# A start in a new order: whole weight rows in one transfer, and landmark sums that begin on GpSimd

## The chip, the cores and the metric

The kernel runs on one core of a Trainium2 chip. The metric is the device time of one execution in microseconds. TensorE (PE), VectorE (DVE), ScalarE (ACT) and GpSimd (POOL) each work through a queue of their own in order; SyncE (SP) issues the transfers.

## The reference

Three stages follow one another: attention with 32 landmarks (Nystrom), then two MLP layers. `w_in` and `w_out` are float64, the rest float32.

```
q, k, v: (4, 8, 576, 64)            # batch, heads, tokens, head width
q_lm, k_lm = means of q, k over 18 neighbouring tokens      # 32 landmarks
A, Bm, C = softmax(q k_lm'), softmax(q_lm k_lm'), softmax(q_lm k')
Z = Bm' / (norm1(Bm) * norminf(Bm) + 1e-6)
6 times: Z = 2 Z - Z Bm Z                                  # Newton
x = (A Z C v) as (2304 tokens, 512)
x = mish(x @ w_in) @ w_out          # 512 -> 2048 -> 512
x = relu(x @ w2_in)**2 @ w2_out     # 512 -> 2048 -> 512
```

## The kernel before

The whole kernel is one list of steps, `PROGRAM`, written out in order. Each step names a thing and a method (`b.sk` is method `sk` of group b); behind @ stands the kind of PSUM tile that the step takes, and `+n` puts n products of the identity with itself on TensorE before it (line 257). Each step issues instructions on one engine, and each engine works through its own in the order of the list; a step waits by semaphore for what it reads and for the buffer that it writes.

*Attention.* a to h are eight groups, each four heads of one of four batches (a, b: batch 0; c, d: batch 1; e to h: batches 2 and 3). `lk`, `lq`, `lv` load k, q and v; every landmark takes 18 tokens, so a partition holds 18 x 64 values. `sk`, `sq` sum the 18 on VectorE (line 471; c to f, whose loads come in two tiles, in two steps, lines 465 and 471), `Sk`, `Sq` copy the sum, `tk`, `tq`, `tl` transpose, `Tk`, `Tq`, `TL` copy that out of PSUM. `pb`, `pc`, `pa` are the score products, `cm ce cr` and `am mi ae su mu` the softmaxes of C and A, `at`, `tb` transposes of A, `ah`, `al` A's high and low part, `pe ET pv cv` the product of C with v.

*Newton.* B0, B1, B2 take a and b, c and d, e to h. `bx be bs nr rs` prepare, `n0` to `n5` are the six rounds on TensorE, each with `r` on ScalarE and `z` on VectorE before the next; `pw`, `wz` multiply the result with `cv`.

*Weights.* U0, U1, ... are units of 128 x 512 float64 values: for each quarter of a layer's 2048 columns four of w_in, then four of w_out (U0 to U3, U4 to U7, and so on). `d` loads a unit, `lo st ab cl ad` build float32 from its two words (ScalarE, VectorE, ScalarE or VectorE, VectorE, GpSimd), `hi`, `lw` split w_out's into a high and a low part. A w_in unit of layer 1 consists of the 64 rows of head c and of head 4 + c, each loaded by a transfer of its own (line 317).

*Layer 1.* Since x = A (Z C v), `w_in` is first multiplied with Z C v: fold `Fbf` (`fo`, line 826; `mh`, `ml`) for batch b and a quarter f of the 2048 columns. A fold is eight products of 64 rows on eight pieces of the array: its two halves of rows (64 each) times its four groups of 32 columns; `g` picks the half of rows and the PSUM bank. Turns t0 to t23 take 384 tokens and a quarter: `f` multiplies A with the fold, `M` is mish, `c`, `g` split, `y` multiplies with w_out, `e` adds up. All such products are made of three, from high and low parts. t0 reads F00 alone, t1 reads F00 and F10.

*Layer 2* (W, K, X, Q, Y, Z steps) follows.

Of the kernel before, what the change touches and what calls it, by code (L numbers as in the profile page):

```python
# [23 lines left out]
LM = 32
SEG = 18
NPB = SEG // 2
# [36 lines left out]
    t0.e0 f.Sk d.su U9.d U11.lo t0.y1 d.mu e.cm f.tl@at t0.e1 f.TL e.ce t0.y2 f.pa@at U11.st c.tb f.at F10.fo@h  # L63
    U11.ab c.ah d.tb f.pc@h e.pa@at t0.e2 f.pb@y f.cm g.lk U11.cl g.lq t0.y3 c.al F10.mh f.ce d.ah d.al F10.ml
    e.pe@h U9.lo e.at U11.ad t0.e3 U9.st U9.ab e.lv U9.cl U9.ad e.ET e.am t1.f0 t1.f1 t1.M0 t1.f2 t1.f3 t1.c0
    g.tk@at g.sk U10.d t1.M1 t2.f0 f.cr g.Tk g.sq t1.g0 t1.c1 g.Sq f.am e.mi f.PB U10.lo t2.f1 U10.st g.tq@at t2.f2
    t1.g1 g.lv t2.M0 g.Sk U10.ab t1.y0 f.pe@h e.ae U13.d U10.cl t1.y1 U10.ad t1.e0 U13.lo e.su U13.st t2.f3 h.lv
# [1321 lines left out]
```

## Time and profile before

| | us |
|---|---|
| time, median of three runs | 791.8 |
| lowest and highest | 791.39, 794.12 |
| span of the profiled execution | 788.7 |
| TensorE busy in it | 764.8 |
| VectorE busy in it | 600.2 |
| GpSimd busy in it | 383.5 |

The profile follows one execution: its span is from its first to its last instruction; a time of its own for that execution, with what lies around the span, is not given, so the median of the runs stands beside it. A busy TensorE is not TensorE at its peak. Idle time of an engine counts only where another waits for that engine.

### The profile page before, as it was taken

The page shows a single profiled execution, that of the slowest core. Times are in us where ns is not written, and L with a number is a line of the kernel's source. Part 1 is how long each engine was busy: PE and PEld are TensorE (multiplying, and loading weights), DVE is VectorE, ACT ScalarE, POOL GpSimd, SP SyncE. Part 2 cuts the span into 40 slices and gives each one's busy share as a digit, 9 for nine tenths or more (in the row PEclk, how much of TensorE's full clock was granted, in tenths as well). Part 3 has the DMA queues.
Part 4 walks back from the last instruction along what each step waited for, and adds up shares of the span by engine and source line. Part 5 has one row for each costly group of instructions (what it writes and reads, how often), then busy time and mean ns, then how long its engine had stood idle before and what let it go on. Part 6 is the DMA issues. An engine that isn't in the chain of part 4 may idle for free.

```text
span 788.7 us, 15310 instructions
## 1 busy us (share of the span) xinstructions
PE 764.8 (97%) x5878; PEld 713.4 (90%) x5878; DVE 600.2 (76%) x937; ACT 369.0 (47%) x582; POOL 383.5 (49%) x273
## 2 busy tenths in 40 slices
...
GB/s 273 299 152 55 205 172 105 58 54 32 103 54 107 121 166 172 190 209 213 205 233 233 248 277 254 259 278 269 265 282 336 351 248 236 218 227 317 329 63 80
DMA packets 87783, 156.71 MB, mean 199 GB/s; under 512 B 9376, under 2 KB 37024, under 8 KB 87712
## 3 DMA queue, kind: packets, MB, share of 16 engines
...
q10 hardware_dynamic: 576, 0.79, 0.4%
...
## 4 chain that ended last, share of the span: by engine, by line
PE 87%; DMA 6%; DVE 4%; ACT 1%; issue 1%; SPq 0%; POOL 0%; DVEq 0%; ACTq 0%; POOLq 0%
PE y L841 8%; PE y L843 8%; PE y L842 8%; PE P L1221 7%; PE P L1222 7%; PE P L1223 7%; DMA rawwi<-in_moe_w_in_dram 4%; PE O L842 4%; PE O L843 4%; PE O L841 4%; PE h L841 4%; PE h L842 4%; PE h L843 4%; PE O L1289 4%; PE O L1290 4%; PE O L1288 3%
## 5 line engine op out<-in xcount | busy, mean ns | idle before, releaser
L1117 POOL TENSOR_TENSOR glr<-A,ghr 128x768 fp32r<-128x768 f32 x49 | 100.3, 2067 | 69.5 <-ACT ghr L1112 69.3
L842 PE MATMUL O<-b,ghr 128*128 128x256 f32 x294 | 83.1, 283 | 0.3 <-DMA b<-sc 0.3
L843 PE MATMUL O<-b,glr 128*128 128x256 f32 x294 | 83.0, 282 | 0.0
L841 PE MATMUL O<-b,ghr 128*128 128x256 f32 x294 | 82.9, 282 | 0.0
L841 PE MATMUL h<-ah,mh 128*128 128x384 f32 (+1 forms) x256 | 78.7, 307 | 0.0
L843 PE MATMUL h<-ah,ml 128*128 128x384 f32 (+1 forms) x256 | 77.9, 304 | 0.0
L842 PE MATMUL h<-al,mh 128*128 128x384 f32 (+1 forms) x256 | 77.9, 304 | 0.0
L1112 ACT CAST ghr<-A 128x768 fp32r<-128x768 f32 x49 | 40.3, 837 | 78.7 <-DVE A L1094 30.2
L955 DVE TENSOR_TENSOR acc<-acc,y 128x384 f32<-128x384 f32 x72 | 39.1, 549 | 42.9 <-PE y L843 42.9
L1251 DVE TENSOR_TENSOR U<-U,P 128x384 f32<-128x384 f32 x72 | 39.7, 552 | 30.7 <-PE P L1223 29.2
L842 PEld LDWEIGHTS O<-b,ghr 128*128 128x128 f32 x294 | 56.0, 191 | 0.6 <-DMA b<-sc 0.6
L843 PEld LDWEIGHTS O<-b,glr 128*128 128x128 f32 x294 | 56.1, 191 | 0.0
L841 PEld LDWEIGHTS O<-b,ghr 128*128 128x128 f32 x294 | 55.9, 190 | 0.0
L914 DVE TENSOR_TENSOR gl<-s,gh 128x768 fp32r<-128x768 f32 x48 | 51.7, 1080 | 3.9 <-ACT gh L904 3.9
L893 ACT ACTIVATE s<-h 128x768 f32<-128x768 f32 x48 | 39.0, 813 | 30.8 <-DVE gl L914 18.1
L841 PEld LDWEIGHTS h<-ah,mh 128*128 128x128 f32 x256 | 48.5, 190 | 3.9 <-issue 1.7
L843 PEld LDWEIGHTS h<-ah,ml 128*128 128x128 f32 x256 | 48.6, 190 | 0.0
L842 PEld LDWEIGHTS h<-al,mh 128*128 128x128 f32 x256 | 48.6, 190 | 0.0
L904 ACT CAST gh<-s 128x768 fp32r<-128x768 f32 x48 | 39.6, 836 | 13.8 <-PE y L843 13.5
L1251 DVE TENSOR_TENSOR A<-U,P 128x384 f32<-128x384 f32 x56 | 30.4, 550 | 20.0 <-PE P L1223 17.6
L348 POOL TENSOR_TENSOR wi<-rawwi 128x512 int32<-128x512 int32 x16 | 18.3, 1148 | 54.6 <-DVE rawwi L342 31.2
L1231 ACT COPY U<-P 128x384 f32<-128x384 f32 x24 | 11.5, 478 | 64.5 <-PE P L1223 50.1
...
## 6 DMA issues: line engine op xcount, KB each, us to landing
b<-sc SPq DMA_DIRECT2D x98, 256.0 KB, 4.5
...
rawwi<-in_moe_w_in_dram SPq DMA_DIRECT2D x48, 256.0 KB, 4.2
...
sc<-sh SPq DMA_DIRECT2D x16, 256.0 KB, 5.0
```

Of the source, the lines that this page charges most:

```text
L841: nc.tensor.matmul(ps, wh, rh, start=start, stop=False)
L842: nc.tensor.matmul(ps, wh, rl, start=False, stop=False)
L843: nc.tensor.matmul(ps, wl, rh, start=False, stop=stop)
L904: nc.scalar.copy(gh, s)
L914: nc.vector.tensor_tensor(self.gl[:, sl, :], self.s[hf], self.gh[:, sl, :].bitcast(F32), ALU.subtract)
L955: nc.vector.tensor_tensor(a, a, ps, ALU.add)
L1112: nc.scalar.copy(self.form(k)[0], self.A[self.src(k)])
L1117: nc.gpsimd.tensor_tensor(lo, self.A[self.src(k)], hi.bitcast(F32), ALU.subtract)
L1221: nc.tensor.matmul(ps[:, :TT], wh[:, c], xh[:, c, :], start=c == 0, stop=False)
L1222: nc.tensor.matmul(ps[:, :TT], wh[:, c], xl[:, c, :], start=False, stop=False)
L1223: nc.tensor.matmul(ps[:, :TT], wl[:, c], xh[:, c, :], start=False, stop=c == 1)
L1251: nc.vector.tensor_tensor(to, x, self.ps[i][:, :TT], ALU.add)
```

## The change

A w_in unit of layer 1 becomes 128 rows in one transfer, so that it holds heads 2c and 2c + 1. `fo` takes its rows accordingly (half of rows `e`, bank `g`), `pw` writes its result in the matching layout with twice as many products of half the width, and `pa` writes group 1's heads in swapped places. New steps `hk`, `hq` add the three thirds of the 18 tokens on GpSimd, and the sum on VectorE then reads 384 values a partition; b to f have both, a, g and h have none. The `+n` come to 23 products where they were 35. The first 1240 steps, now 1250, stand in a new order; the other 1320 are as they were.

The list below is cut after the first product `t0.y0` of either order.

```diff
@@ PROGRAM @@
-    a.lq a.lk b.lk U1.d@m U0.d@m b.lq a.sq a.tq@h d.lq a.Tq a.sk a.tk@h a.Sq a.Sk a.tl@y b.sk U2.d@m a.Tk a.TL
-    a.pa@at U1.lo U4.d U1.st a.pb@y a.pc@h U7.d@gl a.PB b.Sk a.at U0.lo c.lk b.tk@h a.cm a.am a.ce U0.st a.mi b.Tk
-    b.tq@h b.sq U1.ab U0.ab c.lq a.pe@at U1.cl b.Sq b.Tq d.sq b.tl@y U1.ad U3.d@m U2.lo b.TL b.pc@h+4 a.cr a.ET
-    U0.cl U4.lo a.lv U2.st b.pb@at U4.st b.PB b.pa@at B0.bx b.cm B0.be U4.ab c.tk@h+3 a.ae B0.bs U7.lo U6.d@gh U4.cl
-    b.ce d.lk B0.nr@y b.at d.tq@h B0.rs c.tq@at+2 d.Tq b.lv a.su c.Tq b.am U3.lo e.lk B0.n0@at+5 U7.st b.mi c.sq
-    B0.r0 U4.ad c.Tk U2.ab c.Sq B0.z0 c.sk U3.st B0.n1@y B0.r1 B0.z1 b.pe@h a.pv@y B0.n2@at+2 U0.ad U7.ab d.tk@h
-    a.mu c.Sk a.cv b.ET U3.ab B0.r2 U2.cl a.tb c.tl@y b.ae U3.cl B0.z2 d.Sq d.sk c.TL B0.n3@y+2 B0.r3 c.pb@at a.ah
-    U7.cl B0.z3 U3.ad U5.d b.pv@y+1 U6.lo d.Sk c.pc@h b.cr d.Tk c.cm U2.ad B0.n4@y b.cv B0.r4 e.tk@h B0.z4 d.tl@y
-    B0.n5@y c.PB b.su f.lk B0.z5 c.pa@at c.at B0.pw@y+3 U4.hi c.ce c.am B0.wz U7.ad d.TL e.lq a.al U7.hi U7.lw
-    d.pc@at d.lv b.mu d.cm e.Tk b.tb d.ce c.mi d.pb@y e.sq F00.fo@h F00.mh d.pe@at F00.ml f.tk@h+4 U6.st d.PB U4.lw
-    b.ah U5.lo B1.bx d.ET f.lq B1.be f.Tk b.al d.pa@at t0.f0 c.ae t0.f1 d.at B1.bs d.cr B1.nr@y U5.st U6.ab U8.d
-    U5.ab B1.rs t0.M0 c.su t0.f2 U6.cl d.am t0.f3 c.lv B1.n0@y+2 B1.z0 d.pv@y U8.lo U6.ad c.pe@h e.Sq B1.r0 t0.c0
-    e.sk U8.st B1.n1@y B1.z1 f.tq@at t0.M1 e.tq@h d.mi t0.g0 U6.hi B1.r1 B1.n2@y d.cv c.ET B1.z2 U5.cl U5.ad f.Tq
-    B1.r2 e.Tq B1.n3@y+4 B1.r3 c.pv@y c.cr e.Sk B1.z3 t0.c1 f.sq c.cv B1.n4@y+3 U5.hi e.tl@y B1.r4 e.TL B1.z4 U6.lw
-    B1.n5@at e.pc@h U5.lw B1.z5 t0.g1 U8.ab U11.d e.pb@at B1.pw@y f.Sq B1.wz e.PB t0.y0 d.ae U8.cl U8.ad f.sk c.mu
...
+    a.lk a.tk@h a.sk U0.d@m U0.lo a.lq a.tq@h+1 U0.st b.lq U0.ab a.sq b.hq U2.d@m a.Tk U0.cl a.Sk d.lk d.hk b.sq
+    a.Sq c.lq a.tl@y+2 a.Tq b.tq@h a.TL a.pc@h U2.lo b.Tq a.pb@y U2.st a.cm a.pa@at a.at a.am d.sk U2.ab a.ce U2.cl
+    d.tk@h+1 c.hq d.Tk a.PB b.lk b.hk b.sk a.pe@at+1 a.ET U4.d U4.lo b.tk@h b.Tk U4.st c.lk c.tk@h+3 c.sq a.cr c.hk
+    b.Sq b.Sk b.tl@y+1 U4.ab U4.cl b.TL b.pb@at+2 c.sk b.PB c.Tk b.pc@h b.cm U1.d@m U1.lo b.ce b.pa@at+2 B0.bx B0.be
+    a.mi a.ae e.lk e.hk U5.d e.tk@h b.pe@h b.ET b.at c.Sq c.Sk c.tq@at B0.bs B0.nr@y U4.ad U5.lo b.am U1.st B0.rs
+    U5.st c.Tq d.lq d.hq d.sq c.tl@y c.TL d.tq@h B0.n0@at U3.d@m U3.lo U0.ad U4.hi B0.r0 d.Sq b.mi B0.z0 B0.n1@y+1
+    d.Tq U3.st b.cr B0.r1 B0.z1 a.su U4.lw U3.ab b.lv b.pv@y b.cv B0.n2@at B0.r2 B0.z2 c.pc@h a.lv U3.cl U1.ab U1.cl
+    c.pb@at c.PB b.ae B0.n3@y B0.r3 B0.z3 c.pa@at c.at d.Sk d.tl@y d.TL d.pb@y+3 d.PB e.Tk U3.ad B0.n4@y b.su
+    d.pc@at B0.r4 B0.z4 U8.d a.pv@y a.mu U6.d@gh U8.lo a.tb a.ah a.cv d.cm B0.n5@y B0.z5 B0.pw@y+2 d.ce d.pe@at
+    U5.ab B1.bx B1.be c.lv b.mu b.tb b.ah B0.wz U8.st U5.cl d.ET U1.ad U2.ad F00.fo@h F00.mh c.cm c.ce a.al U5.ad
+    F00.ml d.lv d.pv@y e.sk U5.hi d.pa@at d.at b.al t0.f0 t0.f1 U7.d@gl t0.f2 U7.lo B1.bs B1.nr@y t0.M0 d.cr t0.f3
+    d.cv U5.lw t0.c0 B1.rs U7.st f.lk f.hk f.sk e.Sk U6.lo f.lq U6.st B1.n0@y+1 B1.z0 t0.M1 f.tq@at f.hq B1.r0 f.sq
+    c.pe@h B1.n1@y U7.ab B1.z1 B1.r1 f.tk@h c.ET e.lq U7.cl U6.ab B1.n2@y B1.z2 B1.r2 f.Tq c.cr U6.cl e.tq@h B1.n3@y
+    B1.r3 e.hq c.pv@y e.Tq B1.z3 B1.n4@y e.sq B1.r4 U7.ad f.Sk U6.ad B1.z4 B1.n5@at+2 B1.z5 e.Sq e.tl@y U6.hi t0.g0
+    c.cv B1.pw@y+1 e.TL e.pb@at B1.wz t0.c1 t0.g1 U6.lw f.Sq e.PB U7.hi d.am e.lv U7.lw e.pc@h f.Tk e.cm c.am U8.ab
+    f.tl@at U8.cl e.ce f.TL e.cr U11.d U11.lo U11.st t0.y0 t0.e0 f.lv U8.ad t0.y1 U11.ab e.pe@h f.pb@y f.pa@at e.ET
...
@@ -311,13 +311,8 @@
                     for h in range(2):
                         nc.sync.dma_start(dst[:, 1 - h], src[:, h])
             else:
-
-                for g in range(2):
-                    r0 = (4 * g + self.c) * D
-                    nc.sync.dma_start(
-                        flat_[g * D : (g + 1) * D],
-                        W.wi.bitcast(U32)[r0 : r0 + D, self.fg * 2 * DM : (self.fg + 1) * 2 * DM],
-                    )
+                cols = slice(self.fg * 2 * DM, (self.fg + 1) * 2 * DM)
+                nc.sync.dma_start(flat_, W.wi.bitcast(U32)[self.c * P : (self.c + 1) * P, cols])
             self.low, self.up = raw[:, :, 0], raw[:, :, 1]
 
         def lo(self):
@@ -416,7 +411,7 @@
             self.of, self.b, self.g = of, b, g
             self.n = f"{b}{g}"
             self.raws, self.lm, self.T, self.ps, self.v = {}, {}, {}, {}, []
-            self.uses, self.whole = 0, {}
+            self.uses, self.whole, self.spare, self.third = 0, {}, {}, {}
 
         def small(self, nm, shape, bufs=4, tag=None):
             return sm.tile([P] + shape, F32, tag=tag or nm, name=f"{nm}{self.n}", bufs=bufs)
@@ -432,7 +427,9 @@
                 nc.sync.dma_start(r[1], x[:, 6 * P :])
             else:
                 if b == 0:
-                    r = take(tag, [FG * TT], F32, f"{nm}{n}0")[:, : SEG * D]
+                    r = take(tag, [FG * TT], F32, f"{nm}{n}0")
+                    self.spare[nm] = r[:, SEG * D :]
+                    r = r[:, : SEG * D]
                 else:
                     r = take("T", [10 * P], F32, f"{nm}{n}0")[:, : SEG * D]
                 nc.sync.dma_start(r, x)
@@ -455,11 +452,30 @@
                 nc.sync.dma_start(t, v[self.b, h0 : h0 + 2].rearrange("h (p j) d -> p h j d", j=NJ))
                 self.v.append(t)
 
+        def thirds(self, nm):
+
+            r = self.raws[nm]
+            if len(r) > 2:
+                x, room = [r[0][:, : 3 * P], r[0][:, 3 * P :], r[1]], r[2][:, 3 * P :]
+            else:
+                x, room = [self.whole[nm][:, i * 3 * P : (i + 1) * 3 * P] for i in range(3)], self.spare[nm]
+            nc.gpsimd.tensor_tensor(room, x[0], x[1], ALU.add)
+            nc.gpsimd.tensor_tensor(room, room, x[2], ALU.add)
+            self.third[nm] = room
+
+        def hk(self):
+            self.thirds("k")
+
+        def hq(self):
+            self.thirds("q")
+
         def sums(self, nm):
 
             t = take("lmd", [2, D], F32, f"lm{nm}{self.n}")
             r = self.raws[nm]
-            if len(r) > 2:
+            if nm in self.third:
+                whole = self.third[nm]
+            elif len(r) > 2:
 
                 rest = r[2]
                 nc.vector.tensor_reduce(
@@ -616,10 +632,12 @@
             kT, qT = self.T["k"], self.T["q"]
             self.a = ps = big(f"pa{self.n}", tag)
             for h in range(4):
-                hs = slice(h * LM, (h + 1) * LM)
+                hs, to = slice(h * LM, (h + 1) * LM), (h ^ self.g) * LM
                 for t in range(2):
                     ts = slice(t * D, (t + 1) * D)
-                    nc.tensor.matmul(ps[hs, t, :HALF], kT[ts, NPB, hs], qT[ts, :NPB, hs], start=True, stop=True)
+                    nc.tensor.matmul(
+                        ps[to : to + LM, t, :HALF], kT[ts, NPB, hs], qT[ts, :NPB, hs], start=True, stop=True
+                    )
             self.turned()
 
         def at(self):
@@ -794,11 +812,11 @@
 
             self.ps = one(f"pw{self.b}", tag)
             for g in range(self.G):
-                nc.tensor.matmul(
-                    self.ps[g % 2 * D : (g % 2 + 1) * D, g // 2 * P : (g // 2 + 1) * P],
-                    self.cv[:, g, :], self.diag[:, g].rearrange("p h l -> p (h l)"),
-                    start=True, stop=True,
-                )
+                for e in range(2):
+                    nc.tensor.matmul(
+                        self.ps[e * D : (e + 1) * D, g * D : (g + 1) * D], self.cv[:, g, :],
+                        self.diag[:, g].rearrange("p (k e) l -> p e k l", e=2)[:, e], start=True, stop=True,
+                    )
 
         def wz(self):
             n = len(self.all)
@@ -820,10 +838,14 @@
             W, wz = layers[0], next(x.w[self.b] for x in batches if self.b in x.all)
             self.ps = ps = big(f"m{self.b}{self.fg}", tag)
             for h in range(4):
-                hs = slice(h * LM, (h + 1) * LM)
+                k, e = divmod(h, 2)
+                es = slice(e * D, (e + 1) * D)
                 for g in range(2):
-                    gs = slice(g * D, (g + 1) * D)
-                    nc.tensor.matmul(ps[hs, g, :], wz[gs, hs], W.i[self.fg * FG + h][gs, :], start=True, stop=True)
+                    c, to = 2 * g + k, (h ^ g) * LM
+                    nc.tensor.matmul(
+                        ps[to : to + LM, g, :], wz[es, c * LM : (c + 1) * LM], W.i[self.fg * FG + c][es, :],
+                        start=True, stop=True,
+                    )
             if self.b == B - 1:
                 for u in units[self.fg * 2 * FG :][:FG]:
                     u.gone()
```

## Rows read from the trace of the kernel before

**Rows 1.** Page, busy time, share of the span and instructions of each engine.

```profile
PE 764.8 (97%) x5878; PEld 713.4 (90%) x5878; DVE 600.2 (76%) x937; ACT 369.0 (47%) x582; POOL 383.5 (49%) x273
```

**Rows 2.** Windows: stretch, length, each engine's busy us, clock, DMA share, GB/s.

```profile
0.00:30.00 30.00, 18.58 (x186) 14.79 (x186) 23.70 (x46) 16.81 (x32) 3.76 (x13) 0.94 0.97 281
30.00:40.00 10.00, 7.60 (x158) 6.33 (x158) 9.86 (x16) 6.87 (x19) 5.61 (x5) 1.00 0.99 296
0.00:71.40 71.40, 53.73 (x863) 41.28 (x863) 62.04 (x129) 48.84 (x101) 25.09 (x33) 0.98 0.70 201
71.40:100.00 28.60, 28.60 (x250) 26.78 (x249) 25.72 (x41) 22.35 (x42) 12.23 (x12) 1.00 0.68 179
100.00:160.00 60.00, 58.73 (x821) 51.60 (x820) 44.87 (x89) 46.57 (x80) 20.68 (x17) 1.00 0.36 109
160.00:400.00 240.00, 240.00 (x1597) 227.75 (x1596) 176.55 (x276) 130.72 (x181) 93.79 (x65) 1.00 0.42 136
31.50:46.20 14.70, 11.76 (x281) 8.78 (x280) 14.32 (x30) 11.89 (x31) 8.63 (x10) 1.00 0.98 280
55.57:71.00 15.43, 13.69 (x292) 11.06 (x292) 13.27 (x33) 13.07 (x25) 5.75 (x5) 1.00 0.07 18
```

**Rows 3.** Timeline of TensorE: start us, us, line, output<-inputs, instructions.

```profile
31.48 0.43 PE L763 MATMUL nw__412<-inv 32*32 32x64 f32 x16
...
46.18 0.44 PE L797 MATMUL pw<-inv,cv 128*64 128x128 f32 x4
...
53.04 0.44 PE L841 MATMUL h<-ah,mh 128*128 128x384 f32 x1
...
55.57 0.49 PE L730 MATMUL nrm<-inv,bones 128*128 128x128 f32 x2 [0.16 <-DVE rec L581]
...
71.35 0.44 PE L841 MATMUL y<-gh,wo_0h 128*128 128x384 f32 x1
...
146.07 0.65 PE L763 MATMUL nw__2072<-inv 32*32 32x64 f32 x32
...
147.44 0.65 PE L763 MATMUL nw__2105<-inv 32*32 32x64 f32 x32
```

**Rows 4.** Windows, 0 to 80 us, identity products alone (line 257).

```profile
0.00:80.00 80.00, 10.90 (x70) 9.31 (x70) 0.98 0.68 192
```

**Rows 5.** The chain that ended last: start us, us, what held it.

```profile
29.48 6.33 DMA k<-in_k_dram
...
49.18 1.42 DVE q L465
50.62 0.98 DVE lmq L471
```

**Rows 6.** Groups by form, 0 to 120 us, landmark sums: busy us, mean ns.

```profile
L471 DVE TENSOR_REDUCE lmq<-q 128x64 f32<-128x1152 f32 x4 | 8.8, 2188 | 2.8 <-DMA q<-in_q_dram 2.8
L465 DVE TENSOR_REDUCE k<-k 128x64 f32<-128x768 f32 x4 | 6.1, 1530 | 0.0
L471 DVE TENSOR_REDUCE lmk<-k 128x64 f32<-128x448 f32 x4 | 3.8, 962 | 0.1
```

**Rows 7.** Groups by form, 0 to 80 us, GpSimd.

```profile
L348 POOL TENSOR_TENSOR wi<-rawwi 128x512 int32<-128x512 int32 x5 | 5.1, 1037 | 8.8 <-DVE rawwi L342 8.8
L679 POOL TENSOR_TENSOR al<-At,ah 128x384 fp32r<-128x384 f32 x3 | 3.0, 1012 | 0.3 <-ACT ah L675 0.3
```

**Rows 8.** DMA issues, 0 to 120 us, and SP's timeline.

```profile
rawwi<-in_moe_w_in_dram SPq DMA_DIRECT2D x18, 256.0 KB, 6.1
k<-in_k_dram SPq DMA_DIRECT2D x4, 576.0 KB, 4.7
...
2.14 2.49 SPq L317 DMA_DIRECT2D rawwi<-in_moe_w_in_dram  x4
```

**Rows 9.** Windows around a pause of TensorE.

```profile
15.60:18.00 2.40, 2.37 (x14) 2.31 (x15) 2.40 (x3) 2.01 (x3) 1.33 (x1) 0.65 1.02 227
```

**Rows 10.** Timeline of TensorE, one fold.

```profile
190.88 1.09 PE L826 MATMUL m<-wi,wz 64*32 64x512 f32 x16
```

More of the change, by code (lines that the diff above doesn't have):

```diff
@@ L63 @@
[L63 to L67, printed above, removed]
@@ new lines @@
+    f.mi t1.g0 t1.c1 g.lq t1.g1 U13.d U13.lo t1.y1 t2.M0 U10.ab t2.c0 g.sq g.Sq f.ae g.tq@at g.Tq U10.cl U10.ad
+    U13.st U13.ab t1.y0 t1.e0 U13.cl t1.e1 t2.g0 F11.fo@at t2.M1 F01.fo@h U15.d f.su t1.y2 F01.mh t1.e2 t1.y3 g.sk
+    g.Sk g.tl@y U15.lo F01.ml U15.st F11.mh F11.ml g.TL f.pe@h t3.f0 t3.f1 U13.ad U13.hi f.ET t2.c1 t1.e3 e.am
+    g.pa@at U13.lw t3.M0 t3.c0 t4.f0 U15.ab g.at g.pc@at g.cm t2.g1 g.pb@y g.PB g.am g.ce t3.f2 t3.f3 t3.M1 U15.cl
+    U15.ad t3.c1 U15.hi t2.y0 t3.g0 t3.g1 U15.lw h.lk h.tk@at g.mi h.sk t4.f1 t4.f2 t4.M0 h.lq h.Tk t4.f3 t2.e0
@@ new lines @@
+    t22.f0 t20.e0 U38.d t20.y1 t20.e1 t22.f1 X0.h2 t21.M1 Q02.a2 X0.l0 X0.t2 U38.lo t21.c0 t21.c1 t20.y2 t20.y3
+    t22.f2 t21.g0 t22.M0 t22.c0 t22.f3 W6.l0 W6.sv0 U38.st U36.st U36.ab U36.cl t20.e2 U36.ad W6.h1 W6.l1 W7.v0
+    W7.v1 t21.g1 t21.y0 t21.e0 t23.f0 t23.f1 X0.t1 Q00.a0 t22.M1 t22.c1 U38.ab W6.sv1 t20.e3 X0.h5 X0.l5 Q01.a5
+    t21.y1 U38.cl W7.v2 W7.v3 W7.h0 W7.l0 t21.y2 t21.e1 Q00.a5 X0.t3 t22.g0 U39.d t23.f2 X0.l2 Q00.a4 t21.y3 U38.ad
+    t23.M0 t22.g1 U44.d t21.e2 U39.lo t21.e3 t23.f3 W7.h1 W7.l1 t22.y0 U44.lo W7.sv0 t22.y1 t22.e0 W7.sv1 t23.M1
@@ new lines @@
+    U39.st U39.ab K0.t1 t23.c0 x.two t22.y2 U39.cl t22.e1 t23.c1 t23.g0 K0.t3 K0.t2 t22.e2 K0.t4 X0.h6 t23.g1 Q02.a6
+    t22.y3 t22.e3 t23.y0 t23.e0 K0.h0 t23.y1 t23.y2 t23.e1 Q00.a6 t23.y3 K0.h1 X0.h4 U39.ad K0.l1 K0.l0 K0.sv1 U45.d
+    X0.l4 U36.hi X0.l6 X0.l1 K1.t1 U45.lo t23.e2 Q00.p6@h U44.st K0.sv0 U45.st Q01.a6 U36.lw Q00.p1 X0.h3 t23.e3
+    Q00.p2 Q00.p7@at Q01.a2 X0.l3 U45.ab Q00.s Q00.d1 Q01.a1 Q01.a3 Q00.p5@h Q02.a0 K1.t2 Q00.d2 Q00.d3 U45.cl
+    Q00.p4 U36.sv U37.hi U37.lw Q00.d4 Q00.d5 Q00.d6 Q00.p3 U44.ab Q03.a3 Q00.d7 U45.ad Q02.p1 Q00.r0 Q01.p1 Q00.r1
@@ new lines @@
+    K3.l1 Q03.g0 K4.t1 Q05.a5 Q02.y1 Q03.r1 K2.h1 Q04.p6 Q04.s Q02.y4 Q04.p2 K2.sv0 Q06.a3 U46.hi Q03.h1 Q03.g1
+    U55.d U55.lo Q02.y5 K4.t3 U53.hi U54.lo Q04.d1 U46.lw Q04.p7 Q04.d2 Q04.d3 K4.t2 U54.st Q05.p1 Q05.s U54.ab
+    K3.sv1 Q04.p5 K4.t4 U55.st Q05.a4 K1.h1 Q04.p4 X1.h1 Q04.d4 Q04.d5 Q03.y1 K4.h0 Q04.p3 Q07.a3 K1.l1 Q03.y4
+    U46.sv U47.sv Q04.d6 U55.ab Q04.d7 X1.h3 Q05.a3 Q04.r1 Q05.p2 K4.h1 Q04.r0 U53.lw Q04.h0 U54.cl Q06.a5 U55.cl
+    K1.sv1 Q06.a6 Q12.a4 U53.sv U55.ad Q07.a6 K4.l0 Q04.g0 Q05.d1 Q04.h1 Q05.p6 Q05.d2 U61.d U52.hi Q03.y2 K4.sv0
@@ new lines @@
+    Y10.p3@h Q15.d4 Y11.l1 Y11.t4 Q15.p4 Y11.h5 Y11.p4@h K7.sv0 Y11.b7 Q15.d5 Q17.a5 Q15.p3 Y11.l5 Q15.d6 Y10.a6
+    Y11.p2@at Y11.h6 Q17.a0 Y12.r3 Y11.a4 Q16.a3 Y11.l4 Y11.l6 Q16.p1 Y11.a2 Y11.b5 Y12.r0 Y11.p7@h Y11.a7 Q16.s
+    Y11.p6@at Q15.d7 K7.sv1 Y12.b2 Y12.r1 Q16.a6 Q16.a5 Y12.r2 Y11.p5@h Y12.b3 X2.t1 Y12.b0 Q16.a4 X2.t3 Q17.p1
+    Q16.p2 Y12.b12 Q16.a1 Y10.a3 Y12.b13 Q17.a4 Y12.h1 Q17.a3 Q17.a6 Y11.p3@h Y12.h2 Y12.b1 Q17.s Y12.h0 X2.h4
+    Y12.l2 Q16.d1 Y12.b11 Y11.a6 Y12.b7 Y12.l1 Y12.t1 Y11.a3 Q17.p2 Q16.p6 Y12.b6 Q17.d1 Q16.d2 X2.h1 Q17.a1
```

253 lines of the change are left out of this document (116 added, 137 removed).

## The prediction

> **What bounds the kernel now.** First the page's busy times: TensorE is busy 97% of the span [rows 1], so only the time in which it idles or does filler work can be won. Second the windows: where is that time? Up to 71.4 us it is busy 53.73, from there to 400 us all but 1.27 (all of it between 100 and 160 us) [rows 2]. So the loss sits in the start, before the first output product of the first turn (`t0.y0`, 71.35 [rows 3]), and it is 17.7 us of idleness, plus the identity products, which fill 10.9 us of TensorE's time in that stretch [rows 4]. After `t0.y0` TensorE is simply fed; an order of steps there changes nothing as long as it stays fed.
>
> Third, what does the start wait for? To about 40 us the DMA engines are full (share 0.97 to 0.99, 281 then 296 GB/s [rows 2]). Beside that VectorE is the tight engine: 14.32 of 14.70 us through the first batch's Newton rounds, 13.27 of 15.43 through the second's, against 11.76 and 13.69 on TensorE, fillers included [rows 2]. The chain that ended last says the same: a load of k to 35.81, then mostly VectorE, with the landmark sums of e standing on it at 49.18 and 50.62 [rows 5]. A reader should see two limits one behind the other: loads until some 36 us, then VectorE until 71.
>
> The sum is made against the profiled execution: span 788.7 us. The runs shown have their median at 791.8, so 3.1 us lie around the span; I carry them over unchanged.
>
> **The change, part by part.** *Sums.* A landmark sum in two parts costs 1.53 + 0.96 = 2.5 us of VectorE, one over 1152 elements 2.2 [rows 6]. A sum over 384 lies below the smallest row (448 elements, 0.96); on the line through 448 and 768 it is 0.85. Ten sums change: eight of c to f save 1.65 each, two of b 1.35: 15.9 us in all. Ahead of `t0.y0` the old order has eleven sums (4 x 2.2 + 7 x 2.5 = 26.3) and the new one twelve (2 x 2.2 + 10 x 0.85 = 12.9): 13.4 us less. Other steps that the new order places there (U8, for one) put about 1.7 back, so some 11.7 of work go; durations overlap at their ends, so this is about 10.7 of time if VectorE is all that counts.
>
> *GpSimd adds.* Each is 128x384 with two inputs. No such add is shown; the nearest rows are the subtraction of that size, 1.01, and the integer add of 512, 1.04, which scaled by size is 0.78 [rows 7]. I take 0.95, so 1.9 a step and 19 us for ten. GpSimd is busy 25.1 of the first 71.4 us [rows 2]; with 44 it still has room. But its queue is in order, and `b.hk`, `c.hk` and `d.hq` wait for loads in front of the subtractions and weight adds. The price of that is in the chain below.
>
> *Transfers.* The w_in halves have 256 KB each, sixteen units, so sixteen issues fewer. An issue takes 0.62 us of the queue [rows 8]; four such units lie ahead of `t0.f0`. The bytes are the same and the DMA engines already full, so I cost it at nothing: what hides it is the full DMA. Without that cover it would give at most 4 x 0.62 = 2.5 us.
>
> *Identity products.* 35 become 23. At 10.9 / 35 = 0.31 us they are 3.7 us of TensorE less, in a stretch where it idles anyway: 0 to 3.7, taken as 0 of its own, since the chain below counts when its inputs come. Against it: after a pause TensorE's granted clock was 0.65 from 15.6 to 18.0 (partly the 1.2 GHz level), with eight transposes in it [rows 9]. The new order has such gaps while it waits for loads; that is before 30 us, where loads decide. Bound: nothing to 1 us.
>
> *`pw`, `pa`, `fo`.* `pw` has twice the products of half the width, some 0.1 us. `pa` moves outputs to other columns, the same number in each. `fo` has the same eight products on the same eight pieces of the array, in another order: nothing, but see the rivals.
>
> *The order.* First the loads. Counting q, k and v pieces at 0.59 MB (576 KB [rows 8]) and units at 0.52, the old list has 8.96 MB up to and with `d.lk`, which landed at 35.81 [rows 5], when 30 x 0.281 + 5.81 x 0.296 = 10.15 MB had moved [rows 2]: a piece lands when 1.2 MB more than its place in the list have moved. In the new list `d.lq` stands at 7.93 MB, so at 32.3 us; `a.lv` at 9.63, 38.0; `U8` at 10.16, 39.8; `d.lv` at 11.86, 45.6.
>
> Now the chain. TensorE's queue has `d.tq` ahead of the first round `B0.n0`: 32.3 plus a transpose group of 0.9 gives 33.2, against 31.48 now [rows 3]; the start of the rounds is 1.7 later, not sooner. The six rounds to `B0.pw` take 14.7 now, 2.45 each; the shortest round shown is 1.37 [rows 3]. Of the 14.32 VectorE-busy us in them, three two-part sums (c twice, d) are 7.5, and the new order has these finished before. So rounds shorten, though not to the floor: the first waits for `d.hq` and `d.sq` (32.3 + 1.9 + 0.85 = 35.0), a later one for `d.TL` and `e.Tk` on ScalarE, the last product for `U8.lo` ahead of `a.cv`. I take 2.0 a round: `B0.pw` at 45.2 (46.18 now). From there to `t0.f0` it is 6.9 us now (53.04); without `e.sq` ahead of `F00.ml`, which is 2.4 [rows 5], but with `c.cm`, `U5.cl` and GpSimd's `b.al` late in the queue, I take 5.2: 50.4. `d.lv` has landed. The second batch's rounds start (`B1.nr`) 2.5 later, as now: 52.9, against 55.57. To `t0.y0` it is 15.8 now, 13.27 of them VectorE; two old sums in it (4.9) become three new ones (2.6). Bounds 13.5 and 15.8; I take 15.0, since the round's own round trips remain: 67.9 against 71.35. That is 3.4 us sooner. TensorE has by then done about 0.5 us more of its useful work. The 1.27 us of idleness after 100 us I halve, as VectorE is lighter there: 0.6. Sum: 3.4 + 0.5 + 0.6 = 4.5; span 784.2, time 787.3.
>
> **The rivals.** 0.5% of the time, 4.0 us, is about what a measurement can tell from no change; my sum lies just beyond it.
>
> 1. *VectorE decides alone.* If the loads' lead is enough, all 10.7 come through: 791.8 - 10.7 = 781.1. For it: 97% busy in the rounds. Against it: the loads and the round trips above.
>
> 2. *GpSimd takes VectorE's place.* A sum now waits for a GpSimd pair behind other work and loads: `U4.lw` frees the buffer for `U8`, behind which the queue of loads stands with `c.lv` and `d.lv`; `b.al` stands last before `t0.f0`. If `U4.lw` is 4 us late, `d.lv` and `t0.f0` are too, and the gain is gone: 791.5. Against it: 44 us of work in 68.
>
> 3. *Slower: the folds stop overlapping.* Old folds pair each half of rows with its own PSUM bank; the new ones write both halves into the same bank at once. A fold's 16 instructions of 512 columns take 1.09 us [rows 10], 0.85 of them four abreast at 2.4 GHz. If halves that share a bank took turns, only two would run abreast: 8 x 0.213 = 1.7 plus the same tail of 0.24, 1.9, so 0.85 more on each of the fourteen folds after the start, 12 us: 787.3 + 12 = 799.3. It decides from 0.6 us a fold. Against it: the Newton products write one bank from four row groups, and 32 of 64 columns, 0.85 us one after another, took 0.65 with their tail [rows 3].
> The Trainium skill, TensorEngine Tiling (Array Packing), Restrictions and Gotchas, says that different row tiles cannot access the same PSUM bank at the same time, and leaves it to software to keep them apart. By that rule the time is this rival's 799.3; the Newton row does not bear it out.
>
> 4. *The later order starves TensorE.* `t1.f0` needs `c.al` and `d.al`, which end a chain through VectorE, GpSimd and ScalarE. More than 8.5 us of new idleness between 71 and 340 us, where 1.27 is now, would make it slower, say 797.
>
> **How the numbers follow.** My sum: 0.42, its own range 784 to 790 (bounds of the round and of the fold path), so 0.27 faster and 0.15 the same. Rival 1: 0.25, faster. Rival 2: 0.19, of which 0.17 the same and 0.02 slower. Rival 3: 0.08; rival 4: 0.06, 0.05 of it slower and 0.01 the same. Faster 0.52, same 0.33, slower 0.15. The range leaves out rival 3 and the outer parts of 1 and 4: 780.5 to 794.
>
> **What would show it.** Right: `B0.n0` near 33 (later than now), `B0.pw` near 45, `t0.f0` near 50, `t0.y0` near 68; sums at 0.85; adds at 0.95; TensorE full from there; folds still near 1.1. `t0.y0` near 61 is rival 1; VectorE waiting for GpSimd's sums, or `d.lv` after 48, is rival 2; folds of 1.9 us, rival 3; idle TensorE after 75 us, rival 4. I am wrong most simply if rounds run at 1.5 or at 2.5 us: that alone moves the time by 3 either way in each batch.

## The result, and the profile after

The changed kernel takes 797.3 us (median of 12 runs, 796.5 to 801.1) beside 791.6 for the kernel before on the same chip: ratio 1.008, 95% interval 1.0064 to 1.0097. It is 0.8% slower; forecast was 787.3, 0.6% faster, with a range up to 794. The profiled spans are 795.9 and 788.7.

The page's busy times of the changed kernel, which answer to [rows 1], and under them a window of its identity products alone, for [rows 4]:

```profile
PE 766.5 (96%) x5870; PEld 710.3 (89%) x5870; DVE 606.4 (76%) x929; ACT 369.9 (46%) x582; POOL 408.3 (51%) x293
```

```profile
0.00:80.00 80.00, 8.86 (x46) 6.96 (x46) 0.98 0.65 209
```

GpSimd has 25 us more, 21 of them the ten pairs of adds. VectorE has 6 us more, although ten sums shrank; this is the first sign that something else grew. Timeline of TensorE of the changed kernel, the marks of the chain (to be held against [rows 3] and, for the fold, [rows 10]):

```profile
32.52 0.43 PE L781 MATMUL nw__452<-inv 32*32 32x64 f32 x16 [1.06 <-DVE inv L771]
...
45.46 0.45 PE L816 MATMUL pw<-inv,cv 128*64 128x64 f32 x8
...
46.98 1.96 PE L845 MATMUL m<-wi,wz 64*32 64x512 f32 x16
...
50.84 0.44 PE L863 MATMUL h<-ah,mh 128*128 128x384 f32 x1
...
55.19 0.49 PE L748 MATMUL nrm<-inv,bones 128*128 128x128 f32 x2 [0.75 <-DVE rec L597]
...
71.20 0.42 PE L863 MATMUL y<-gh,wo_0h 128*128 128x384 f32 x1
...
194.61 1.09 PE L845 MATMUL m<-wi,wz 64*32 64x512 f32 x16
```

Up to `t0.f0` (50.84) the change is 2.2 us ahead of [rows 3]; at `t0.y0` (71.20) 0.15 are left. So nothing is lost at the start, and nothing won. Where do the 7 us go? The first weight load of the second layer lies in a part of the list that is the same in both. Timelines of the weight loads, first of before, then of after:

```profile
417.94 0.19 PEld L1221 LDWEIGHTS P<-fh,q00w 128*128 128x128 f32 x1
```

```profile
425.56 0.19 PEld L1243 LDWEIGHTS P<-fh,q00w 128*128 128x128 f32 x1
```

It is 7.6 us late, and the end 7.2. The whole loss thus lies between 71 and 425 us, where the kernel before was fed without a gap but 1.27 us [rows 2]. Windows of after:

```profile
71.40:100.00 28.60, 27.25 (x236) 24.59 (x235) 21.54 (x38) 22.89 (x40) 15.11 (x14) 1.00 0.51 139
100.00:160.00 60.00, 59.94 (x785) 52.89 (x787) 40.13 (x78) 44.50 (x76) 18.52 (x15) 1.00 0.30 100
160.00:400.00 240.00, 236.37 (x1623) 222.08 (x1622) 184.41 (x281) 131.01 (x184) 93.71 (x66) 1.00 0.40 131
400.00:430.00 30.00, 28.49 (x162) 27.67 (x161) 24.71 (x32) 10.76 (x16) 22.95 (x16) 1.00 0.69 224
```

TensorE idles 6.55 us here (1.35 + 0.06 + 3.63 + 1.51), 5.3 more than before. Between `t0.y0` and that load 7.8 us are lost, so 2.5 more stand as busy time: a product of the `y` kind is drawn 0.34 us long though the next one starts after 0.17, so the first 0.17 of a wait hide behind it, and the first product after a wait is drawn 0.44; 0.27 for each wait, so 2.2 for the eight, an estimate. TensorE's timeline, all rows behind 72 us with over 0.15 us of idle time ahead of them (in brackets, with what ended it):

```profile
79.59 0.72 PE L638 MATMUL pa<-qT,kT 64*32 64x288 f32 x16 [0.93 <-DVE As L648]
...
91.30 0.44 PE L863 MATMUL h<-ah,mh 128*128 128x384 f32 x1 [0.42 <-ACT s L915]
...
180.70 0.36 PE L863 MATMUL h<-ah,mh 128*128 128x192 f32 x1 [1.18 <-ACT s L915]
...
293.48 0.44 PE L863 MATMUL y<-gh,wo_8h 128*128 128x384 f32 x1 [1.44 <-DVE acc L977]
...
335.44 0.44 PE L863 MATMUL y<-gh,wo_8h 128*128 128x384 f32 x1 [0.49 <-DVE acc L977]
...
342.79 0.45 PE L863 MATMUL y<-gh,wo_8h 128*128 128x384 f32 x1 [0.52 <-DVE acc L977]
...
407.96 0.45 PE L863 MATMUL y<-gh,wo_12h 128*128 128x384 f32 x1 [0.96 <-DVE acc L977]
...
415.05 0.45 PE L863 MATMUL y<-gh,wo_12h 128*128 128x384 f32 x1 [0.55 <-DVE acc L977]
```

Five of eight wait for `acc` (step `e`): VectorE adds a finished `y` to its sum and so frees one of the two PSUM tiles of that kind. Why is it late? VectorE's timeline ahead of the longest:

```profile
288.50 1.95 DVE L336 TENSOR_SCALAR rawwi<-rawwi 128x512 f32<-128x512 f32 x1
290.48 2.49 DVE L337 TENSOR_SCALAR rawwi<-rawwi 128x512 uint32<-128x512 uint32 x1
292.89 0.54 DVE L977 TENSOR_TENSOR acc<-acc,y 128x384 f32<-128x384 f32 x1
```

and GpSimd's at the same time (`W1.l0`, `W1.l1`, low halves of a pair of w_in units):

```profile
288.20 1.96 POOL L1004 TENSOR_TENSOR wa<-wa,wh 128x768 fp32r<-128x768 f32 x1 [4.50 <-DVE ws L992]
290.12 2.56 POOL L1004 TENSOR_TENSOR ws<-ws,wh 128x1024 fp32r<-128x1024 f32 x1
```

The two instructions of `U40.cl` take 0.43 us elsewhere. Here they run 1.95 and 2.49, and each ends 0.3 us or less after a GpSimd instruction does (290.16, 292.68). Behind them stands `t13.e1`, and behind that TensorE. The kernel before has the same stretching at the same place; its timeline of VectorE:

```profile
286.96 0.55 DVE L955 TENSOR_TENSOR acc<-acc,y 128x384 f32<-128x384 f32 x1
287.43 1.83 DVE L341 TENSOR_SCALAR rawwi<-rawwi 128x512 f32<-128x512 f32 x1
289.29 2.51 DVE L342 TENSOR_SCALAR rawwi<-rawwi 128x512 uint32<-128x512 uint32 x1
```

but its list says `W1.h1 t13.e1 U40.cl`, where the new one says `U40.cl t13.e1`: the addition (286.96) runs ahead of the slow pair (287.43). Counted over both timelines to 428 us, VectorE rows that are over 1.35 times and 0.25 us longer than the shortest of their kind are 38 before and 57 after, 33.8 and 44.9 us above it in all, and each of them overlaps an instruction of GpSimd. But 13 of the 57 lie ahead of 71 us, where the kernel before has none. Behind it the two differ little, 38 and 44; what differs there is which steps stand behind the slow ones.

### The profile page after: what moved, and what is told of

The parts are those of the page before. It is cut to its first block, busy times and chain, and to the rows that moved or that the text cites. A ratio compares the mean times of both kernels' runs of the same rounds, so it can differ in the third digit from the quotient of the medians.

```text
span 795.9 us, 15267 instructions
## 1 busy us (share of the span) xinstructions
PE 766.5 (96%) x5870; PEld 710.3 (89%) x5870; DVE 606.4 (76%) x929; ACT 369.9 (46%) x582; POOL 408.3 (51%) x293
## 4 chain that ended last, share of the span: by engine, by line
PE 79%; DVE 10%; DMA 5%; issue 3%; ACT 2%; POOL 1%; SPq 0%; DVEq 0%; POOLq 0%; ACTq 0%
PE P L1243 7%; PE P L1244 7%; PE P L1245 7%; PE y L863 7%; PE y L864 6%; PE y L865 6%; PE O L864 4%; PE O L865 4%; PE O L863 4%; PE h L863 4%; PE O L1311 3%; PE O L1312 3%; PE O L1310 3%; PE h L865 3%; PE h L864 3%
## 5 line engine op out<-in xcount | busy, mean ns | idle before, releaser
L1139 POOL TENSOR_TENSOR glr<-A,ghr 128x768 fp32r<-128x768 f32 x49 | 100.5, 2071 | 69.5 <-ACT ghr L1134 69.4
L350 POOL TENSOR_TENSOR wa<-rawwi 128x512 int32<-128x512 int32 x16 | 18.9, 1181 | 44.8 <-DVE rawwi L337 39.6
L357 POOL TENSOR_TENSOR rawwo<-rawwo 128x512 int32<-128x512 int32 x16 | 19.7, 1236 | 43.1 <-DVE rawwo L337 37.7
```

The source lines that it names most:

```text
L1139: nc.gpsimd.tensor_tensor(lo, self.A[self.src(k)], hi.bitcast(F32), ALU.subtract)
```

## The experiments

Three questions: which part of the change loses the time, what makes the evictions late, and what became of the start. The theory at the outset: the order behind `t0.y0` loses. The rivals: the adds on GpSimd, or the layout.

**e1, the layout alone.** The code of the change with `PROGRAM` of the kernel before.

> The changed code (a w_in unit as 128 rows in one transfer, the turned folds, pa and pw) with the order of steps and the identity products of the kernel before, and no adds on GpSimd. Theory: the 5.7 us were lost by the order of the steps behind t0.y0, which leaves TensorE idle for 6.5 us there; the layout costs nothing, so this runs as the kernel before, 790 to 793 us. Rival (the layout): the two row halves of a fold or the larger transfers cost the time; then this shows the loss by itself, 796 to 798 us. If the larger transfers land sooner and that is worth something in any order, 787 to 790 us.

790.4 us, ratio 0.999 (0.9977 to 1.0002). Layout, larger transfers and the new folds cost nothing and give nothing.

**e2, e3, the two halves of the order.** In lists of steps (`new` without `hk`, `hq` in e3):

```diff
-PROGRAM = new
+PROGRAM = new[ahead of t0.y0] + [s for s in old if s not yet done]     # e2
+PROGRAM = old[ahead of t0.y0] + [s for s in new if s not yet done]     # e3
```

> The changed kernel with its new order only up to the first second-layer product of the first tile (t0.y0); the steps that are left follow in the order of the kernel before. All ten pairs of adds on GpSimd are in the part that is kept. Theory (the order behind t0.y0 loses): the starts are level (t0.y0 at 71.2 against 71.35 us), so this runs as the kernel before or up to 1.5 us sooner or later at the seam, 790 to 793 us, with under 2 us of idle TensorE from 72 to 420 us. Rival (the adds on GpSimd, by what they delay): the loss stays, 796 to 798 us.

> The other half: the order of the kernel before up to t0.y0, then what is left in the new order, without adds on GpSimd (all landmark sums on VectorE), with the 128-row transfers. Theory (the order behind t0.y0 loses): 795 to 799 us, with some 5 us of idle TensorE between 72 and 420 us. Rival (the adds on GpSimd): no adds, no loss, 790 to 793 us. Third possibility: the waits of the new order come from how its own start leaves the engines, and then this has neither, 790 to 793 us too, and e2 tells which of the two it is.

e2: 791.0, ratio 1.0004 (0.9991 to 1.0018). e3: 802.3, 1.0152 (1.0127 to 1.0176). With the old order behind `t0.y0` the loss is gone; with the new one it is there even without one add on GpSimd. Window of e2, 160 to 400 us:

```profile
160.00:400.00 240.00, 240.00 (x1596) 227.75 (x1595) 175.01 (x275) 130.71 (x181) 94.00 (x65) 1.00 0.41 136
```

In e3 TensorE is busy 236.54 us of these 240, with the waits at the same products, 1.18, 1.43, 0.35, 0.50 and, behind 400, 0.96 and 0.54 us long. It is slower than forecast, as its start is late too: `t0.y0` comes at 74.7, and TensorE idled 2.4 of the 3.3 us ahead of it. From there to 100 us it is busy 25.28 of 25.30.

**e4, no adds on GpSimd.**

```diff
-    ... d.lk d.hk b.sq ... c.sq a.cr c.hk
+    ... d.lk b.sq ... c.sq a.cr          # all ten hk, hq dropped
```

> The changed kernel with its whole new order but without the adds on GpSimd: the ten sums are single VectorE sums over 1152 columns again (2.19 us in place of 0.96). Theory (the order behind t0.y0 loses, the adds save VectorE time at the start): t0.y0 comes 2 to 6 us later than 71.2, and the time is 798 to 802 us. Rival (the adds on GpSimd cost the time, by what they delay or by a shared port): 791 to 795 us, with a t0.y0 that is no later.

805.8, ratio 1.02 (1.0176 to 1.0223); `t0.y0` at 80.3, both later than forecast (the sums are those of the kernel before, eight of the ten in two parts). The adds don't lose the time: in this order they bring 8.5 us (805.8 less 797.3; 9.5 by the ratios). Some of that may be TensorE's clock: the granted mean from 0 to 80 us is 0.88 in e4's profile, and 0.98 from 0 to 71 in the changed kernel's.

**e5, ten steps moved** to mend the eight waits.

```diff
-U11.cl f.at ... U10.lo c.al U10.st ... t1.M1 ... t6.f2 ... h.ah t6.M0 t6.c0
+f.at U11.cl ... c.al ... t1.M1 U10.lo U10.st ... t6.f2 t6.M0 t6.c0 ... h.ah
-U40.cl t13.e1 ... W4.v0 ... F13.ml t16.e1 ... t16.y3 t16.e3 ... t16.e2
+t13.e1 U40.cl ... t16.e1 W4.v0 ... F13.ml ... t16.y3 t16.e2 t16.e3
-X0.l2 ... t21.e2 ... U39.cl t22.e1
+t21.e2 X0.l2 ... t22.e1 U39.cl
```

> The changed kernel with nine steps moved by a few places, each one named by a wait of TensorE behind 75 us in its trace: a PSUM eviction (f.at, t13.e1, t16.e1, t16.e2, t21.e2, t22.e1) or a Mish (t6.M0, and t1.M0 by way of U10.lo) goes ahead of the weight steps that stood before it on VectorE or ScalarE. Theory (the loss is these eight waits, 6.5 us of idle TensorE and some 0.2 us more behind each): they go, 789 to 792 us. Rival (the later order is bound by the sum of VectorE's work, so the next wait takes the place of each): idle TensorE stays over 4 us behind 75 us, 795 to 798 us.

793.7, ratio 1.0032 (1.0017 to 1.0047): more than half of the 0.8% comes back, but not all. The waits named are gone but for 0.2 us; new ones have come, seen in e5's waits of TensorE from 71 to 430 us (what waited for what: us, times, longest):

```profile
PE y L864 <- DVE gl L936: 2.1, 2, 1.6
PE y L863 <- ACT fh L1038: 0.5, 1, 0.5
...
PE h L863 <- ACT s L915: 0.2, 1, 0.2
```

So the rival was half right: moving steps leaves the stretching in place, and another step stands behind it.

**e6, e7, the stretching itself.** The order is untouched; `l`, the low halves of the second layer's w_in pairs on GpSimd, is changed. e6 leaves three quarters of these columns out; e7 does all of them.

```diff
+            n //= 4                                   # e6: a quarter of the columns
             nc.gpsimd.tensor_tensor(flat(t)[:, :n] ...
+            for c in range(0, n, 256):                # e7: all, 256 at a time
+                nc.gpsimd.tensor_tensor(flat(t)[:, c : c + 256] ...
```

> The changed kernel in its own order; of the second layer's w_in pairs GpSimd subtracts only the first quarter of the columns for the low halves (192 or 256 of 768 or 1024), and the others stay as they were, so part of the computation is left out. It asks whether the late evictions come from where they stand or from GpSimd's long instructions, behind whose end VectorE's own stretch. Theory (GpSimd holds a port): VectorE's 1.95 and 2.49 us at 288 to 293 fall to about 0.4, its 2.4 us at 331, 340 and 401 too; TensorE's waits at 293.5, 335.4, 342.8 and 408 go, those at 79.6, 91.3 and 180.7 stay; 792 to 794.5 us. Rival (the place in the queue alone): the waits stay, 796 to 798 us.

> The changed kernel in its own order, with the same subtractions for the low halves of the w_in pairs as three or four GpSimd instructions of 256 columns in place of one of 768 or 1024. If a VectorE instruction waits only for the GpSimd instruction that runs, and comes in between two pieces, its longest falls from 2.5 to about 1.1 us and TensorE's four waits between 290 and 410 us shrink by 2 to 3 us together: 793.5 to 796 us. If GpSimd keeps VectorE out over all the pieces, the waits stay: 796.5 to 798 us, or more if the pieces cost GpSimd time.

e6: 792.2, ratio 1.0004 (0.9988 to 1.0021). e7: 795.0, 1.0044 (1.0027 to 1.0061). VectorE's timeline of e6, then of e7, at the place shown above:

```profile
286.50 0.71 DVE L336 TENSOR_SCALAR rawwi<-rawwi 128x512 f32<-128x512 f32 x1
287.24 0.43 DVE L337 TENSOR_SCALAR rawwi<-rawwi 128x512 uint32<-128x512 uint32 x1
```

```profile
289.07 0.85 DVE L336 TENSOR_SCALAR rawwi<-rawwi 128x512 f32<-128x512 f32 x1
289.95 0.85 DVE L337 TENSOR_SCALAR rawwi<-rawwi 128x512 uint32<-128x512 uint32 x1
```

With GpSimd's instructions cut to a quarter all five waits for `acc` are gone (the one at 415 too, which had not been forecast), and those at 79.6 and 180.7 stay as said (0.94, 1.18). The one at 91.3 was to stay too and is gone; it is missing in e9 as well, where nothing behind `t0.y0` was changed. In pieces, with all the work done, a VectorE instruction waits for one piece at most: 0.85 in place of 1.95 and 2.49. The waits for `acc` shrink from 4.0 to 1.0 us. The price is on GpSimd, whose timeline in e7 has 5.4 us for both (4.5 in one piece each):

```profile
288.77 2.62 POOL L1006 TENSOR_TENSOR wa<-wa,wh 128x256 fp32r<-128x256 f32 x3 [4.31 <-DVE ws L992]
291.35 2.82 POOL L1006 TENSOR_TENSOR ws<-ws,wh 128x256 fp32r<-128x256 f32 x4
```

**e11, both remedies** (e5's list with e7's pieces).

> The changed kernel with the nine moved steps of e5 and with GpSimd's low halves in pieces of 256 columns as in e7: both remedies of the late evictions together. Theory (what is left in e5, 4 us of idle TensorE behind 75 us, is the same stretching of VectorE's instructions at other places): 790 to 792.5 us, idle under 2.5 us. Rival (what is left has another cause): no better than e5, 793 to 795 us.

791.1, ratio 0.9996 (0.998 to 1.0012). By the median the loss is gone; from 160 to 400 us TensorE is busy 240.00 of 240 again. The start moves with more than these remedies (see the part on it below), so here are the two marks of each profile by themselves, in us: `t0.y0` and the first weight load of the second layer, with the same work between them. From that load to the end it is 369.8 to 370.8 in all.

| | `t0.y0` | load | between |
|---|---|---|---|
| before | 71.35 | 417.94 | 346.6 |
| after | 71.20 | 425.56 | 354.4 |
| e1, layout alone | 72.03 | 418.79 | 346.8 |
| e2, old order behind | 70.15 | 417.69 | 347.5 |
| e3, new order behind | 74.68 | 428.11 | 353.4 |
| e5, steps moved | 69.32 | 420.35 | 351.0 |
| e6, a quarter of `l` | 69.38 | 418.00 | 348.6 |
| e7, `l` in pieces | 72.17 | 423.40 | 351.2 |
| e11, both | 71.38 | 418.83 | 347.5 |

Of the 7.8 us, e5 and e7 bring back 3.3 and 3.1, both together 6.9, and e6 5.7. So the order behind `t0.y0` decides, and most of its price comes by the stretching.

**e8, the adds in the old order.** `hk`, `hq` right behind their `lk`, `lq` in the list of before.

> The order and the identity products of the kernel before, with the 128-row transfers and with the ten pairs of adds put right behind the load of their data, so that ten VectorE sums of 2.2 to 2.5 us become 0.83. In the new order these adds bring t0.y0 9 us sooner (80.3 against 71.2). Theory (VectorE decides the start in either order): t0.y0 from 72 to 66 to 69 us, and with no loss behind it 786 to 789 us. Rival (GpSimd's queue, in order, stands at the adds for loads that come late and holds back the weight adds and alow parts behind them): t0.y0 not sooner, 790 to 795 us.

795.2, ratio 1.0049 (1.0032 to 1.0067), 4.8 us slower than e1, which differs in the adds alone; `t0.y0` at 75.8. The rival holds, just past its range. Rows of GpSimd, VectorE and TensorE of e8, in order of time:

```profile
29.82 0.99 POOL L462 TENSOR_TENSOR k<-k 128x384 f32<-128x384 f32 x1 [3.39 <-DMA k<-in_k_dram]
...
36.16 1.34 POOL L659 TENSOR_TENSOR As<-As,mxa 128x576 f32<-128x576 f32 x1
...
40.82 0.78 DVE L678 STREAM_TRANSPOSE At<-As 128x576 f32<-128x576 f32 x1 [3.03 <-POOL As L673]
...
42.55 0.42 PE L781 MATMUL nw__540<-inv 32*32 32x64 f32 x16 [3.60 <-DVE inv L798]
```

GpSimd stands 3.39 us for a load of k and 1.77 for the next (up to 33.66), so its work on `As` behind them starts at 36.16, where e1 has it at 29.36. VectorE waits 3.03 for the last of it with the Newton step behind it, and TensorE 3.60. So 1.35 to 1.65 us saved on VectorE in each of ten sums bring 8.5 us in one order and cost 4.8 in the other.

**e9, more identity products at the start.**

```diff
-B0.nr@y ... B0.n0@at ... B0.n1@y+1 ... B0.n2@at ... B0.n5@y
+B0.nr@y+3 ... B0.n0@at+4 ... B0.n1@y+3 ... B0.n2@at+2 ... B0.n5@y+6
```

> The changed kernel in its own order with 17 more identity products in five pauses of the first batch's rounds (nr, n0, n1, n2, n5), so 40 in place of 23. Kernels with this same start showed t0.y0 at 69.3 us where the granted clock stayed at 1.00 from 28 to 50 us and at 70.2 to 72.2 where it fell to 0.50 to 0.69 in some of these us. Theory (the pauses without products cost clock): the clock stays at 1.00 from 28 to 50, t0.y0 at 69.0 to 69.8, and the time is 1 to 2 us under the changed kernel's, 795 to 796.5 us. Rival (the products stand in the way of useful ones, or the clock falls all the same): t0.y0 at 71 or later, 797 to 799 us.

796.7, ratio 1.007 (1.0048 to 1.0092): not to be told from the changed kernel. Windows of after, then of e9:

```profile
42.00:44.00 2.00, 0.29 (x12) 0.13 (x2) 1.17 (x3) 1.62 (x6) 2.00 (x3) 1.00 1.09 254
46.00:50.00 4.00, 4.00 (x70) 1.89 (x69) 2.98 (x7) 2.67 (x6) 1.72 (x2) 0.57 1.00 353
```

```profile
42.00:44.00 2.00, 1.36 (x35) 1.14 (x27) 1.41 (x3) 1.60 (x5) 2.00 (x3) 1.00 1.10 253
46.00:50.00 4.00, 3.51 (x94) 2.03 (x94) 3.88 (x11) 2.88 (x6) 0.96 (x1) 1.00 0.91 318
```

In the changed kernel's profile TensorE was busy 0.29 of 2 us, and from 46 to 50 the granted clock was 0.57, for the most part its 1.2 GHz level. With the products it stays full, as forecast, but `t0.y0` is at 70.2, not 69.0 to 69.8. They seem to stand in the way themselves: `B0.pw` comes at 46.3, where e5 and e6, with a full clock and without them, have it at 44.8 and 45.3.

**e10, e12, a faster version?** e2's list with e9's products and the seam mended; e12 moves `f.pa` and `f.at` ahead too.

```diff
-U11.st c.mi c.ae c.su d.mi t0.y0 d.ae U8.ad c.mu t0.e0 d.su U9.d t0.y1 d.mu t0.e1
+U11.st t0.y0 c.mi t0.y1 t0.e0 c.ae t0.e1 c.su d.mi d.ae U8.ad c.mu d.su U9.d d.mu
```

> The kernel of e2 (new start, order of the kernel before from t0.y0 on) with the same 17 more identity products, and with t0.y0, t0.y1 and their evictions t0.e0 and t0.e1 ahead of the steps c.mi and c.ae, behind whose ScalarE work the eviction stood in e2 (TensorE waited 1.8 us for it at 76.4). Theory (the start of the change gains some 2 us where the clock holds and nothing is lost behind it): 787 to 789.5 us, faster than both kernels by 0.3 to 0.5%. Rival (the two us come back at the next wait): 790 to 792 us.

> The kernel of e10 with f.pa one product group earlier (ahead of t0.y2) and the eviction f.at ahead of d.su on VectorE: in e10 TensorE waited 1.25 us at 80.1 for that eviction, which stood behind d.su, d.mu's reciprocal and c.tb. Theory (each such wait behind the start is worth its length, since TensorE is full after it): the wait goes, 788 to 789 us, 0.3 to 0.4% under the kernel before. Rival (the next wait takes its place): 789 to 790.5 us, as e10.

789.5, ratio 0.9977 (0.9963 to 0.9991), and 789.5, 0.9978 (0.9962 to 0.9993). Both are faster than the kernel before, by 0.2%; e12's step gives nothing beyond e10, and its profile shows why: a wait of 0.98 us for `acc` on ScalarE at 80.4 has taken the place of the 1.25.

## Why the prediction was wrong

**The step that failed** is the sentence "After `t0.y0` TensorE is simply fed; an order of steps there changes nothing as long as it stays fed". It was true of before, and taken over for a list with some thousand steps in other places. In its place the runs showed that the same work behind `t0.y0` takes 354.4 us in the new order and 346.6 in the old one, and 353.4 with the old start ahead of it (e3). The second term that failed is the 3.4 us of the start, of which 0.15 came. Rival 4 named the outcome (797, by new idleness) and got 0.06; its place and cause were others, though: `t1.f0` did not wait for `c.al` or `d.al`. The idleness sits at PSUM evictions and a Mish queued behind weight steps. For the five waits for `acc`, 4.0 of the 6.5 us, these steps are long because GpSimd runs beside them (e6, e7, e11). The one at 79.6 looks alike: `U11.cl` ahead of `f.at` has an instruction of 0.43 us that takes 1.27, beside GpSimd work that e6 and e7 leave as it is. The Mish at 180.7 (1.2 us) stands behind steps of ScalarE. Both go in e5, which moves steps. VectorE's busy share of 67 to 82% in that stretch did not show it: a mean says nothing of a queue in which 0.9 us of work can take 4.4.

**The start.** Right to 0.7 us are `B0.n0` (33.2; 32.5), `B0.pw` (45.2; 45.5) and `t0.f0` (50.4; 50.8), the first two by luck. `B0.n0` was to wait for d's q, landing at 32.3; but the loads moved 406 GB/s from 10 to 20 us where the working had 281, GpSimd's `d.hq` began on that q at 25.64, and `B0.n0` waited for VectorE (the row at 32.52 above). `B0.pw` came right because a start 0.7 sooner made up for rounds of 2.16 us, not 2.0. And the lead of the loads was lost again: SyncE's queue stood 11.0 us for `U4.lw` on GpSimd, which rival 2 had named, and from 28 to 33 us the DMA engines were all but idle. GpSimd's timeline, SyncE's waits from 0 to 46 us (what waited for what: us, times, longest) and a window, of after:

```profile
25.64 1.05 POOL L462 TENSOR_TENSOR q<-q 128x384 f32<-128x384 f32 x1
```

```profile
SPq L315 <- POOL wo_0l L375: 11.0, 1, 11.0
```

```profile
28.00:33.00 5.00, 2.82 (x49) 2.23 (x48) 4.80 (x13) 3.60 (x9) 2.88 (x3) 1.00 0.07 19
```

What these loads would be worth without that stop was not tried. Wrong are `B1.nr` (52.9; 55.2) and `t0.y0` (67.9; 71.2), the 3.4 us term. Other kernels with the same list up to there had `t0.y0` at 69.3 and 69.4 with a full clock (e5, e6), and at 71.4 and 72.2 with a clock of 0.50 to 0.69 in parts of 34 to 50 us (e11, e7). So some 1.9 of the 3.3 us come with the clock (no run sets it apart), for which the working had "nothing to 1 us", and only before 30 us. In the changed kernel's profile two things make them up: the first fold runs 1.96 in place of 1.09 us, so that VectorE's step behind it begins at 50.09 (48.93 in e5), and VectorE, now later, meets the new adds, where an instruction of 0.17 us takes 0.75. `B1.nr` is then 1.8 us behind e5's. A second such instruction, 0.93 us long, comes after `B1.nr` and adds nothing that is left at `t0.y0`, which is 16.0 us behind `B1.nr` in both. Timeline of VectorE, then GpSimd's, of after:

```profile
52.97 0.75 DVE L737 TENSOR_SCALAR sb<-sb 128x2 f32<-128x2 f32 x1
...
56.88 0.93 DVE L765 TENSOR_SCALAR c<-c 128x2 f32<-128x2 f32 x1
```

```profile
52.68 1.01 POOL L462 TENSOR_TENSOR k<-k 128x384 f32<-128x384 f32 x1
```

In e5, VectorE starts the first of them at 51.82, 0.11 us ahead of the add (51.93), and both take 0.17. The other 1.4 us are 0.5 too few up to `nr` (53.4 in e5) and 1.0 in the rounds, 16.0 us from there, above the upper bound of 15.8; what holds the rounds was not tried.

**Right in mechanism.** A sum over 384 takes 0.83 (0.85); an add on GpSimd 1.06 on the mean of all twenty (0.95); groups by form of after:

```profile
L487 DVE TENSOR_REDUCE lmk<-k 128x64 f32<-128x384 f32 x5 | 4.2, 834 | 0.0
...
L462 POOL TENSOR_TENSOR q<-q 128x384 f32<-128x384 f32 x5 | 5.5, 1105 | 7.6 <-DMA q<-in_q_dram 7.6
```

Transfers at nothing: e1, though full DMA engines did move more (see the end). Identity products near nothing: with 17 more, e9 can't be told from the change. The idleness of 100 to 160 us went from 1.27 to 0.06, more than the 0.6 credited.

**The rivals.** 1, VectorE alone: no; ten sums took 1.3 us and more less each, and `t0.y0` came 0.15 sooner. 2, GpSimd in VectorE's place: its queue of loads did stand, but d's v was in at 46.6, and `t0.f0` came in time; in e8 it is what happens. 3, folds: no; a fold takes 1.09 as in [rows 10], and e1 runs them at no loss. The Trainium skill's rule on row tiles and a PSUM bank (TensorEngine Tiling (Array Packing), Restrictions and Gotchas) has no price here.
